# Two pairs' first rows at the head of an attention and feed-forward kernel on one core

## The chip, the cores and the metric

The kernel runs on 1 core of one Trainium2 chip. The metric is device microseconds of one execution, the median of several. TensorE's clock is shown by the profile as the share that the throttle granted, 1.00 for 2.4 GHz and 0.50 for 1.2 GHz.

## What is computed

The attention has 4 batches, 8 heads, 576 positions and 64 columns to a head. A decay that follows from `f` is added to the scores, so that each position fades with distance:

```python
log_f = np.log(np.clip(f, 0.0001, 1.0))
cum = np.cumsum(log_f, axis=-1)
scores = scale * q @ k.T + cum[:, :, :, None] - cum[:, :, None, :]   # then the causal mask
attn = softmax(scores);  x = (attn @ v) laid out as 2304 rows of 512
x = relu(x @ w_in1)**2 @ w_out1          # 512 -> 2048 -> 512
x = elu(x @ w_in2) @ w_out2              # 512 -> 2048 -> 512
```

## The kernel before

All four stages are in one program. The attention is done two heads (a pair) at a time. A pair has five steps, which the list `todo` holds: `("A", 0)` and `("A", 1)` are the first 256 rows of its two heads, `("4", 0)` the last 64 rows of both heads together, and `("B", 0)` and `("B", 1)` the 256 rows between, for one head each. Here A00 is step A of pair 0, head 0, and B11 is step B of pair 1, head 1. A step has a first half, `soft` (scores on TensorE, row minimum on VectorE, exponentials on ScalarE with their sums) and a second half, `outs` (transposes of the exponentials on TensorE, copies of them on ScalarE, the product with the values, and after the second head of a pair the division by the sums, `norm_x`, and the split of the result, `store_x`). `LAG = 1` puts the second half one turn of the loop behind the first.

Batch 0 is "plain": its scores are one fp32 product over 68 rows, 64 of q and k and 4 that carry the decay. Those four rows are the decay rows. For the 256 first rows they are taken straight from the tile `ca`; for the other rows they go out to the DRAM tensor `aug` (`aug_rows`, five writes) and are read back into the operand tiles. Of each batch 0 head the kernel loads q and k (320 KB), values (160 KB) and decay rows (20 KB); of pair 0 it loads ahead of that a 256 KB piece, `first`, and a 128 KB piece, `firstv`, which is what its A steps need.

The first feed-forward layer's weights come as 64-bit numbers in 16 pieces of 512 KB. `stage` asks for the next piece, and `words` turns one into fp32: an absolute value on ScalarE (L150), four operations on VectorE (L151 to L154), then a rounding copy on ScalarE (L170) and a subtraction on VectorE (L119). `W_AT` says how many pieces are converted in each turn of the loop. 256 tokens at a time (a unit) go through that layer, and its matmuls are put between the attention's steps by a running credit (`fill`). Unit 0 can begin when the last A step of batch 0 is done and converted weights are there; its first matmul in the profile is at 91.74 us.

All loads and stores go by the queue of SyncE. `queued` ties each of batch 0's loads behind the one before it, so that their order is the program's. The order of the rest on each engine comes from a planner that runs when the program is built; `issue_after` adds ties to it. Engines take their instructions in the order so made.

While unit 0 hasn't begun, `fill` gives TensorE products of a zero tile (L255): 46 of them at the very start, and two or three after each half step in the first `FILL_TO` turns, which makes 54 more in the kernel before. Buffers that matter: `raw` has 3, `ea` (exponentials of A) 2, `eb` (exponentials of B) 3, `xA` one. The tiles `cp` and `cn`, from which `aug_rows` writes, hold two of the three `eb` buffers until turn 8 (`AUG1`), when the rows of the other batches are written.

Of the kernel before, what the change touches and what calls it, by code (L numbers as in the profile page):

```python
# [22 lines left out]
Q0, Q4 = 448, 320  # L23
QW = 704
RAW = QW + S
ALL = RAW + 5 * D
# [6 lines left out]
W_MAX = float(np.uint32(0x47EFFE00).view(np.float32))  # L33
PACE = (1.5, 1.5, 1.5, 1.5)
COST = {'A': 0.7, '4': 1.1, 'B': 1.7}
W_AT = (1, 1, 0, 1, 1, 0, 0, 1, 2, 1, 0, 0, 1, 2, 1, 0, 0, 1, 2, 1)
AHEAD = 2
FETCH = 4
LAG = 1
HOLD = 8  # L40
KEPT = 0

PLAIN = (0,)

# [11 lines left out]
OPS = 7  # L56


WARM, FILL, FILL_TO = 46, 2, 6
AUG1 = 8  # L60
DELAY = 0
MEM = "gpsimd"
# [7 lines left out]
def f32(ap):  # L70
    return ap.bitcast(F32)
# [10 lines left out]
def attention_then_moe_kernel(ctx, tc, first, firstv, plain, qkv, aug0, f, w1, w2, out):  # L82
    nc = tc.nc
# [11 lines left out]
    aug = dram.tile([B * H, 4, RAW], F32, name="aug")  # L95
# [36 lines left out]
        nc.gpsimd.tensor_tensor(out=dst, in0=x, in1=f32(hi), op=ALU.subtract)  # L132

    staged = []
    to_stage = [(fc, i) for i in range(2) for fc in range(8)]

    def stage():
        if not to_stage:
            return
        fc, i = to_stage.pop(0)  # L140
        n = n_raw[0] % 5
        n_raw[0] += 1
        raw = raws_w[:, n] if n < 2 else a1.tile([128, 512, 2], I32, tag="qk2", name="wraw1", bufs=3)
        queued(raw, w1[fc, i].bitcast(I32).rearrange("p (n t) -> p n t", t=2), len(to_stage) > 10)
        staged.append(raw)

    def words(raw):
        lo, hi = raw[:, :, 0], raw[:, :, 1]
        t = xa.tile([128, 512], I32, tag="o", name="wt")
        nc.scalar.activation(out=f32(t), in_=f32(hi), func=AF.Abs)  # L150
        nc.vector.tensor_scalar(f32(t), f32(t), W_MIN, W_MAX, op0=ALU.max, op1=ALU.min)  # L151
        nc.vector.tensor_scalar(t, t, 3, 0x3FFFFFFF, op0=ALU.logical_shift_left, op1=ALU.bitwise_and)
        nc.vector.scalar_tensor_tensor(t, hi, -0x40000000, t, op0=ALU.bitwise_and, op1=ALU.bitwise_or)  # L153
        nc.vector.scalar_tensor_tensor(t, lo, 29, t, op0=ALU.logical_shift_right, op1=ALU.bitwise_or)  # L154
        return t
# [102 lines left out]

    raws = {}

    pairs = {}

    def fetch_head(b, h, part):
        if b in PLAIN:
            fetch_plain(b, h, part)
# [7 lines left out]
    def queued(out, in_, hold=True):  # L273
        if last_dma[0] is None:
            last_dma[0] = nc.sync.dma_start(out=out, in_=in_)
            return
        with tc.issue_after(last_dma[0].ins):
            d = nc.sync.dma_start(out=out, in_=in_)
        if hold:
            last_dma[0] = d  # L280

    def fetch_first(t):
        queued(t[0:64, 0:1024], first)
        stage()
        for i in range(2):
            queued(t[64:68, 512 * i:512 * i + 512], f32(ca[i:i + 1]))
        queued(t[:, 1024:1280], firstv)

    def fetch_plain(b, h, part):
        g = b * H + h  # L290
        k = h % 2
        if part == "A":
            if k == 0:
                t = ab.tile([128, ALL], F32, tag="raw", name="rawA", bufs=BUFS["raw"])
                fetch_first(t)
                pairs[b, h // 2] = t
            t = pairs[b, h // 2]
            raws[b, h, part] = Plain(t, 512 * k - Q0, 512 * k + 256, t[:, 1024 + 128 * k:1152 + 128 * k].rearrange("p (j d) -> p j d", d=D))
            return
        if k == 0:  # L300
            t = ab.tile([128, ALL], F32, tag="raw", name="rawB", bufs=BUFS["raw"])
            v = t[:, RAW:ALL]
        else:
            t = hd.tile([128, RAW], F32, tag="qk1", name="rawC", bufs=BUFS["qs"])
            v = hd.tile([128, 5 * D], F32, tag="vv", name="vp", bufs=BUFS["vv"])
        queued(t[0:64, 0:RAW], plain[h])
        queued(v, qkv[b, h, :, RAW:ALL])
        if g >= 2:
            nc.sync.dma_start(out=t[64:68, 0:RAW], in_=aug[g])
        else:  # L310
            late_aug.append((t, g))
        raws[b, h, part] = Plain(t, 0, QW, v.rearrange("p (j d) -> p j d", d=D))

    late_aug = []

    def aug_split():
        cp, cn = (ab.tile([32, 2, S - 256], F32R, tag="eb", name=t, bufs=BUFS["eb"]) for t in ("cp", "cn"))
        split_c(cp, cn, slice(256, S))
        return cp, cn
# [54 lines left out]
        nc.vector.tensor_tensor_reduce(out=e, in0=s, in1=m, scale=-0.125, scalar=init, op0=ALU.add, op1=ALU.min, accum_out=nm)  # L374

    def expo(e, nm, z):
        nc.scalar.activation(out=e, in_=e, func=AF.Exp, bias=nm, scale=-1.0, accum_out=z)

    def invert(z, r):
        nc.vector.tensor_scalar(z, z, 1e-9, None, op0=ALU.add)  # L380
# [56 lines left out]
    def tr(dst, src, c0=0):  # L437
        seen[0] = nc.tensor.transpose(dst, src, ident[:, c0:c0 + 128])  # L438
# [33 lines left out]
    def store_x(b, hp, x, c0, n):  # L472
# [224 lines left out]
    loads = []  # L697
    for i, (b, hp, kind, k) in enumerate(todo):
        if (b, hp) == (0, 0):
            if kind == "A":  # L700
                loads.append((i, b, hp, k, "A"))
            elif kind == "4":
                loads += [(i + 2, b, hp, 0, "B"), (i + 2, b, hp, 1, "B")]
        elif kind == "A":
            loads.append((i, b, hp, k, "F"))

    fetches = [(i if part == "F" else 0, b, 2 * hp + k, part) for i, b, hp, k, part in loads]

    def ready(u):
        b, s = divmod(u * CH + CH - 1, S)  # L710
# [477 lines left out]
```

## Time and profile before

| | |
|---|---|
| three runs | 1048.82, 1050.67, 1051.39 us; median 1050.67 |
| profiled execution | 1046.67 us, its span 1044.8 us, granted clock 0.99 on average |
| busy share of the span | TensorE 98%, VectorE 67%, ScalarE 50%, GpSimd 26% |
| zero products (L255) | 100, the first at 1.05 us, the last at 53.2 us |
| first scores of A00, of the step 4 of pair 0, of unit 0 | 10.0, 21.3, 91.7 us |

TensorE is busy nearly throughout by this account, but the ends of matmuls are modelled, and a slice in which it runs at half clock counts as busy too. So the share of an engine has to be read with the number of its instructions and with the granted clock, and for each stretch by itself.

### The profile page before, as it was taken

To read this page: it belongs to the slowest core of one execution; us is meant where nothing else is said; L and a number is where in the kernel's file an instruction comes from. 1 tells how busy PE (TensorE), PEld (TensorE's weight loads), DVE (VectorE), ACT (ScalarE), POOL (GpSimd) and SP (SyncE) were. 2 spreads that over 40 slices of the span, in tenths; PEclk is the share of its full clock that TensorE was granted. 3 is DMA by queue.
4 is the path that set the end of the run, shared out by engine and by line. 5 is a ranking of instruction groups with operands and counts; after the bars stand their busy time and mean duration, and the time that the engine had idled before them with its cause. 6 is when DMAs were issued, how large, how long until landed. Compare 5 with 4: busy or idle time off the path is not lost.

```text
span 1044.8 us, 17562 instructions
## 1 busy us (share of the span) xinstructions
PE 1025.5 (98%) x6372; PEld 903.4 (86%) x6372; DVE 702.9 (67%) x1569; ACT 526.1 (50%) x1207; POOL 267.2 (26%) x284
## 2 busy tenths in 40 slices
PE   7999999999999999999999999999999999999998
PEld 6655899999999998889988888988998988899987
DVE  5799478686876338756384869886454989745554
ACT  3677667676767425433253544464343565433331
POOL 2137768777764230004011240210000000000000
PEclk8799999999999999999999999999999999999999
DMA  6955643645441173435264565644324464544502
GB/s 180 244 155 160 191 147 118 189 161 164 155 150 51 42 246 105 127 91 191 76 207 152 190 222 184 216 166 182 101 81 141 143 239 144 162 155 119 171 21 81
DMA packets 73161, 157.23 MB, mean 150 GB/s; under 512 B 9196, under 2 KB 34156, under 8 KB 73044
## 3 DMA queue, kind: packets, MB, share of 16 engines
q1 hardware_dynamic: 73076, 156.13, 46.5%
q8 instruction: 50, 0.82, 0.3%
q14 instruction: 35, 0.29, 0.1%
HBM read 113.98 MB, written 39.22 MB: 147 GB/s over the span
## 4 chain that ended last, share of the span: by engine, by line
PE 84%; DVE 8%; DMA 3%; issue 1%; ACT 1%; POOL 1%; SPq 0%; ACTq 0%; DVEq 0%; POOLq 0%
PE O L183 29%; PE P L183 15%; PE pH L183 11%; PE o L183 7%; PE ph L183 6%; PE pt L438 4%; PE pv L445 4%; PE s L366 2%; PE s L370 2%; PE s L371 2%; PE pv L442 2%; DMA x<-yl 1%; DVE wt L154 1%; DVE wt L153 1%; PE idle L255 1%
## 5 line engine op out<-in xcount | busy, mean ns | idle before, releaser
L183 PEld LDWEIGHTS P<-xu,v 128*128 128x128 f32 x1536 | 200.5, 189 | 11.2 <-DMA xu<-x 1.1
L183 PE MATMUL P<-xu,v 128*128 128x256 f32 x1536 | 204.0, 282 | 0.7 <-DMA xu<-x 0.7
L183 PE MATMUL O<-v,gh 128*128 128x512 f32 x576 | 169.2, 393 | 1.0 <-ACT gh L1003 1.0
L183 PE MATMUL pH<-xu,w 128*128 128x512 f32 (+1 forms) x672 | 140.9, 360 | 0.0
L183 PEld LDWEIGHTS pH<-xu,w 128*128 128x128 f32 x672 | 113.8, 188 | 19.9
L183 PE MATMUL O<-gh,w 128*128 128x512 f32 (+1 forms) x448 | 122.2, 362 | 0.0
L183 PEld LDWEIGHTS O<-v,gh 128*128 128x128 f32 x576 | 102.9, 188 | 18.8 <-ACT gh L1003 1.2
L183 PE MATMUL O<-v,gl 128*128 128x512 f32 x288 | 100.9, 393 | 0.0
L183 PEld LDWEIGHTS O<-gh,w 128*128 128x128 f32 x448 | 79.8, 189 | 14.0
L1032 ACT ACTIVATE hs<-P 128x256 f32<-128x256 f32 x128 | 48.1, 380 | 83.3 <-PE P L183 82.7
L132 POOL TENSOR_TENSOR yl<-pr,yh 128x512 fp32r<-128x512 f32 x18 | 24.5, 1361 | 246.2 <-ACT yh L852 169.9
L132 POOL TENSOR_TENSOR qk<-raw,qk 64x576 fp32r<-64x576 f32 (+1 forms) x48 | 77.7, 1619 | 21.5 <-DVE qk L127 9.7
L1035 DVE TENSOR_TENSOR hs<-P,hs 128x256 f32<-128x256 f32 x96 | 40.4, 422 | 59.6 <-PE P L183 57.4
L183 PE MATMUL O<-gl,w 128*128 128x512 f32 (+1 forms) x224 | 79.9, 363 | 0.0
L183 PE MATMUL o<-gh,w 128*128 128x256 f32 x384 | 75.6, 289 | 0.0
L183 PE MATMUL ph<-xu,w 128*128 128x256 f32 x480 | 67.4, 287 | 0.7 <-ACT g L605 0.7
L1057 ACT ACTIVATE g<-g 128x512 f32<-128x512 f32 x64 | 40.2, 628 | 54.2 <-DVE g L1049 32.3
L610 ACT ACTIVATE gh<-g 128x512 fp32r<-128x512 f32 (+1 forms) x80 | 46.8, 586 | 39.9 <-DVE g L609 35.9
L609 DVE TENSOR_TENSOR g<-g 128x512 f32<-128x512 f32 (+1 forms) x56 | 44.1, 787 | 31.0 <-ACT g L605 30.8
L1003 ACT ACTIVATE gh<-g 128x512 fp32r<-128x512 f32 x72 | 45.4, 631 | 34.4 <-DVE g L1058 27.5
L183 PEld LDWEIGHTS ph<-xu,w 128*128 128x128 f32 x480 | 60.9, 191 | 1.2 <-ACT g L605 0.9
L183 PEld LDWEIGHTS O<-v,gl 128*128 128x128 f32 x288 | 52.8, 188 | 9.9
(155 smaller groups left out, 2067.2 us busy)
## 6 DMA issues: line engine op xcount, KB each, us to landing
xu<-x SPq DMA_DIRECT2D x66, 512.0 KB
wraw<-in_w_dram SPq DMA_DIRECT2D x57, 512.0 KB
raw<-in_qkv_dram SPq DMA_DIRECT2D x24, 800.0 KB
x<-yh SPq DMA_DIRECT2D x31, 256.0 KB
x<-yl SPq DMA_DIRECT2D x31, 256.0 KB
x<-xs SPq DMA_DIRECT2D x16, 320.0 KB
xu<-x SPq DMA_DIRECT2D x16, 256.0 KB
raws_w<-in_w_dram SPq DMA_DIRECT2D x7, 512.0 KB
```

The lines of the kernel that those rows point to most:

```text
L132: nc.gpsimd.tensor_tensor(out=dst, in0=x, in1=f32(hi), op=ALU.subtract)
L183: nc.tensor.matmul(out=dst, lhsT=l, rhs=r, start=first and i == 0, stop=last and i == n - 1, skip_group_check=skip)
L366: seen[0] = nc.tensor.matmul(out=dst, lhsT=hh.t[0:68, hh.q + q0:hh.q + q0 + 128], rhs=hh.t[0:68, hh.k + j0:hh.k + j0 + n], start=first, st ...
L370: nc.tensor.matmul(out=dst, lhsT=qk1[:, q0:q0 + 128], rhs=qk1[:, QW + j0:QW + j0 + n], start=first, stop=False)
L438: seen[0] = nc.tensor.transpose(dst, src, ident[:, c0:c0 + 128])
L445: seen[0] = nc.tensor.matmul(out=dst, lhsT=hh[2][:, J, :], rhs=hl[i], start=first and i == 0, stop=last and i == 1)
L609: (nc.vector if sq == "v" else nc.gpsimd).tensor_tensor(out=g[:, 0:n], in0=g[:, 0:n], in1=g[:, 0:n], op=ALU.mult)
L610: nc.scalar.activation(out=gh[:, 0:n], in_=g[:, 0:n], func=AF.Copy)
L1003: nc.scalar.activation(out=gh, in_=g, func=AF.Copy)
L1032: nc.scalar.activation(out=o, in_=x, func=AF.Copy)
L1035: nc.vector.tensor_tensor(o, y, x, op=ALU.add)
L1057: nc.scalar.activation(out=gs[i], in_=gs[i], func=AF.Exp)
```

## The change

The A steps of two pairs (`EARLY = 2`) come first, then steps 4, B, B of pair 0 and of pair 1; the other pairs keep their order. To feed that, `first` and `firstv` are held for both pairs (the host concatenates them), and the start is written out in `fetch_start`: loads that wait for no computation stand ahead of the decay rows of A, and the second piece of weights ahead of the q, k and values of head 1. `W_AT` is spread differently, with the same 16 pieces in the first 20 turns and 8 of them in the first ten; the absolute value of a piece (L150) is tied behind the last exponentials traced before it; the transposes in `norm_x` of batch 0 are tied behind the last matmul traced; and the zero products stop after four turns of the loop instead of six.

```diff
-W_AT = (1, 1, 0, 1, 1, 0, 0, 1, 2, 1, 0, 0, 1, 2, 1, 0, 0, 1, 2, 1)
+W_AT = (1, 0, 1, 0, 1, 1, 1, 1, 1, 1, 0, 1, 1, 1, 1, 0, 1, 1, 1, 1)
+EARLY = 2
-WARM, FILL, FILL_TO = 46, 2, 6
+WARM, FILL, FILL_TO = 46, 2, 4
@@ words
-        nc.scalar.activation(out=f32(t), in_=f32(hi), func=AF.Abs)
+        if last_exp[0] is None:
+            nc.scalar.activation(out=f32(t), in_=f32(hi), func=AF.Abs)
+        else:
+            with tc.issue_after(last_exp[0].ins):
+                nc.scalar.activation(out=f32(t), in_=f32(hi), func=AF.Abs)
@@ fetch_first, fetch_plain
-    def fetch_first(t):
-        queued(t[0:64, 0:1024], first)
-        stage()
-        for i in range(2):
-            queued(t[64:68, 512 * i:512 * i + 512], f32(ca[i:i + 1]))
-        queued(t[:, 1024:1280], firstv)
+    def load_a(t, hp):
+        queued(t[0:64, 0:1024], first[hp])
+    def rows_a(t, hp):
+        for i in range(2):
+            queued(t[64:68, 512 * i:512 * i + 512], f32(ca[2 * hp + i:2 * hp + i + 1]))
+    def values_a(t, hp):
+        queued(t[:, 1024:1280], firstv[hp])
+    def load_b(h):
+        t, v = whole[h]
+        queued(t[0:64, 0:RAW], plain[h])
+        queued(v, qkv[0, h, :, RAW:ALL])
+    def rows_b(h):
+        queued(whole[h][0][64:68, 0:RAW], aug[h])
+    def fetch_start():
+        queued(aug[0:H], aug0[0:H])
+        ta = tile_a(0)
+        load_a(ta, 0)
+        stage()
+        values_a(ta, 0)
+        tb = tile_a(1)
+        load_a(tb, 1)
+        tile_b(0)
+        load_b(0)
+        values_a(tb, 1)
+        rows_a(ta, 0)
+        rows_a(tb, 1)
+        stage()
+        tile_b(1)
+        load_b(1)
+        aug_rows(slice(0, H), *cpn)
+        stage()
+        for h in range(2):
+            rows_b(h)
+        while len(staged) < 5:
+            stage()
@@ expo
-        nc.scalar.activation(out=e, in_=e, func=AF.Exp, bias=nm, scale=-1.0, accum_out=z)
+        last_exp[0] = nc.scalar.activation(out=e, in_=e, func=AF.Exp, bias=nm, scale=-1.0, accum_out=z)
@@ norm_x
-            tr(pr[:, i * 128:i * 128 + 128], rb[:, i])
+            if b == 0:
+                with tc.issue_after(seen[0].ins):
+                    tr(pr[:, i * 128:i * 128 + 128], rb[:, i])
+            else:
+                tr(pr[:, i * 128:i * 128 + 128], rb[:, i])
@@ todo, loads
-    todo = [(b, hp, kind, k) for b in range(B) for hp in range(H // 2)
-            for kind, k in (("A", 0), ("A", 1), ("4", 0), ("B", 0), ("B", 1))]
+    both, rest = (("A", 0), ("A", 1)), (("4", 0), ("B", 0), ("B", 1))
+    todo = [(0, hp, *s) for part in (both, rest) for hp in range(EARLY) for s in part]
+    todo += [(b, hp, *s) for b in range(B) for hp in range(H // 2) for s in both + rest if b or hp >= EARLY]
-        if (b, hp) == (0, 0):
+        if b == 0 and hp < EARLY:
...
@@ the loop, turn 0
-            queued(aug[0:H], aug0[0:H])
             cpn = aug_split()
+            fetch_start()
...
-        if i == 0:
-            stage()
-            aug_rows(slice(0, H), *cpn)
-            for t, g in late_aug:
-                queued(t[64:68, 0:RAW], aug[g])
-            while len(staged) < 5:
-                stage()
```

## Rows read from the trace of the kernel before

**Rows 1.** Stretch, length, busy us of PE, PEld, DVE, ACT, POOL; clock, DMA share, GB/s

```profile
9.98:21.32 11.34, 6.94 (x35) 4.78 (x35) 5.88 (x17) 4.83 (x15) 0.60 (x2) 0.93 0.68 165
21.32:38.43 17.11, 17.11 (x51) 12.06 (x51) 8.55 (x23) 7.26 (x16) 2.00 (x2) 0.55 1.03 260
38.43:91.74 53.31, 51.86 (x248) 31.20 (x247) 48.94 (x130) 40.92 (x110) 20.12 (x24) 1.00 0.63 190
...
110.00:300.00 190.00, 187.23 (x1472) 179.99 (x1472) 138.97 (x403) 131.13 (x355) 141.40 (x146) 1.00 0.51 157
```

**Rows 2.** Waits of VectorE from 10 to 92 us, the longest

```profile
DVE wt L151 <- ACT wt L150: 6.4, 2, 3.6
```

**Rows 3.** Timeline of ScalarE: start us, us, what, idle before and its releaser

```profile
6.99 0.67 ACT L150 ACTIVATE wt<-raws_w 128x512 f32<-128x512 f32 x1
...
17.96 0.66 ACT L150 ACTIVATE wt<-raws_w 128x512 f32<-128x512 f32 x1 [3.49 <-DMA raws_w<-in_w_dram]
...
18.79 0.47 ACT L123 ACTIVATE ea<-pt 128x384 f32<-128x384 f32 x1
```

**Rows 4.** Timeline of all engines, the decay rows and what they release

```profile
7.91 1.41 SPq L278 DMA_DIRECT2D rawA<-ca  x2
...
10.01 1.10 PE L366 MATMUL s<-rawA 68*128 68x256 f32 x4 [0.96 <-DMA rawA<-ca]
...
14.83 0.27 SPq L278 DMA_DIRECT2D aug<-cn  x1
...
18.98 0.25 SPq L278 DMA_DIRECT2D rawB<-aug  x1
...
21.32 2.26 PE L366 MATMUL s<-rawB 68*128 68x288 f32 x4 [0.90 <-DVE xA L470]
```

**Rows 5.** Chain of waits from 18 to 26 us, in order of time

```profile
18.65 0.44 DVE wt L151
...
20.30 0.69 DVE wt L154
...
21.34 4.16 PE s L366 x8
```

**Rows 6.** Busy time and clock in stretches of 2 us, columns as in rows 1

```profile
8.00:10.00 2.00, 1.05 (x9) 0.86 (x9) 1.93 (x7) 0.00 (x0) 0.00 (x0) 1.00 0.02 6
...
14.00:16.00 2.00, 1.95 (x11) 1.15 (x10) 0.18 (x1) 0.47 (x3) 0.60 (x2) 1.00 1.05 234
...
18.00:20.00 2.00, 0.69 (x3) 0.54 (x4) 1.28 (x3) 1.25 (x3) 0.00 (x0) 0.94 0.03 8
...
34.00:36.00 2.00, 2.00 (x12) 2.00 (x10) 0.18 (x1) 0.45 (x2) 0.00 (x0) 0.50 1.01 182
36.00:38.00 2.00, 2.00 (x10) 1.37 (x10) 0.85 (x2) 1.93 (x4) 0.00 (x0) 0.79 1.12 200
```

**Rows 7.** Timeline of VectorE: first row minimum of B00 and of B01

```profile
28.73 0.69 DVE L374 CUSTOM_DVE_ANT_0 eb<-s,mz 128x512 f32<-128x512 f32 x1 [1.85 <-PE s L366]
...
38.43 0.69 DVE L374 CUSTOM_DVE_ANT_0 eb<-s,mz 128x512 f32<-128x512 f32 x1 [0.54 <-PE pt L438]
```

**Rows 8.** Groups by line, 10 to 92 us: busy us, mean ns of one, idle before

```profile
L374 DVE CUSTOM_DVE_ANT_0 eb<-s,mz 128x512 f32<-128x512 f32 (+1 forms) x13 | 7.9, 623 | 3.5 <-PE s L366 3.0 <-PE pt L438 0.5
...
L377 ACT ACTIVATE ea<-ea,nm 128x256 f32<-128x256 f32 (+1 forms) x16 | 7.1, 448 | 1.4 <-DVE nm L374 1.4
...
L374 DVE CUSTOM_DVE_ANT_0 ea<-s,mz 128x256 f32<-128x256 f32 (+1 forms) x16 | 5.1, 349 | 0.9 <-PE s L366 0.9
...
L377 ACT ACTIVATION_READ_ACCUMULATOR ea<-ea,nm 128x1 f32 x16 | 3.1, 192 | 0.0
...
L123 ACT ACTIVATE ea<-pt 128x384 f32<-128x384 f32 x6 | 2.9, 479 | 1.1 <-PE pt L438 1.1
...
L123 ACT ACTIVATE xA<-pv 64x256 f32<-64x256 f32 x6 | 2.2, 367 | 1.3 <-PE pv L442 1.2
...
L374 DVE CUSTOM_DVE_ANT_0 e<-s,m,nm 128x288 f32<-128x288 f32 x4 | 2.0, 503 | 0.0
```

More of the change, by code (lines that the diff above doesn't have):

```diff
@@ L134, in attention_then_moe_kernel @@
     staged = []
+    last_exp = [None]
     to_stage = [(fc, i) for i in range(2) for fc in range(8)]
@@ L259, in attention_then_moe_kernel @@
     raws = {}
-    pairs = {}
     def fetch_head(b, h, part):
         if b in PLAIN:
-            fetch_plain(b, h, part)
+            fetch_plain(h)
             return
@@ L280, in queued @@
             last_dma[0] = d
-    def fetch_first(t):
-        queued(t[0:64, 0:1024], first)
-        stage()
-        for i in range(2):
-            queued(t[64:68, 512 * i:512 * i + 512], f32(ca[i:i + 1]))
-        queued(t[:, 1024:1280], firstv)
[L289 to L300, printed above, removed]
+    whole = {}
@@ new lines, in tile_a @@
+    def tile_a(hp):
+        t = ab.tile([128, ALL], F32, tag="raw", name="rawA", bufs=BUFS["raw"])
+        for k in range(2):
+            raws[0, 2 * hp + k, "A"] = Plain(t, 512 * k - Q0, 512 * k + 256,
+                                             t[:, 1024 + 128 * k:1152 + 128 * k].rearrange("p (j d) -> p j d", d=D))
+        return t
+    def load_a(t, hp):
+        queued(t[0:64, 0:1024], first[hp])
+    def rows_a(t, hp):
+        for i in range(2):
+            queued(t[64:68, 512 * i:512 * i + 512], f32(ca[2 * hp + i:2 * hp + i + 1]))
@@ L301, in fetch_plain, with tile_b @@
+    def values_a(t, hp):
+        queued(t[:, 1024:1280], firstv[hp])
+    def tile_b(h):
+        if h % 2:
+            t = hd.tile([128, RAW], F32, tag="qk1", name="rawC", bufs=BUFS["qs"])
+            v = hd.tile([128, 5 * D], F32, tag="vv", name="vp", bufs=BUFS["vv"])
+        else:
             t = ab.tile([128, ALL], F32, tag="raw", name="rawB", bufs=BUFS["raw"])
             v = t[:, RAW:ALL]
-        else:
-            t = hd.tile([128, RAW], F32, tag="qk1", name="rawC", bufs=BUFS["qs"])
-            v = hd.tile([128, 5 * D], F32, tag="vv", name="vp", bufs=BUFS["vv"])
+        whole[h] = t, v
+        raws[0, h, "B"] = raws[0, h, "F"] = Plain(t, 0, QW, v.rearrange("p (j d) -> p j d", d=D))
@@ L306, in fetch_plain @@
+    def load_b(h):
+        t, v = whole[h]
         queued(t[0:64, 0:RAW], plain[h])
[L307 to L314, printed above, removed]
+        queued(v, qkv[0, h, :, RAW:ALL])
[23 more added lines that the diff above has]
+            stage()
@@ L316, in aug_split, with fetch_plain @@
+    def fetch_plain(h):
+        tile_b(h)
+        load_b(h)
+        rows_b(h)
     def aug_split():
@@ L468, in norm_x @@
         for i in range(2):
-            tr(pr[:, i * 128:i * 128 + 128], rb[:, i])
+            if b == 0:
+                with tc.issue_after(seen[0].ins):
+                    tr(pr[:, i * 128:i * 128 + 128], rb[:, i])
+            else:
+                tr(pr[:, i * 128:i * 128 + 128], rb[:, i])
         nc.vector.tensor_tensor(x[:, c0:c0 + 256], x[:, c0:c0 + 256], pr[:, 0:256], op=ALU.mult)
@@ L692, in weights @@
             yield
-    todo = [(b, hp, kind, k) for b in range(B) for hp in range(H // 2)
-            for kind, k in (("A", 0), ("A", 1), ("4", 0), ("B", 0), ("B", 1))]
+    both, rest = (("A", 0), ("A", 1)), (("4", 0), ("B", 0), ("B", 1))
+    todo = [(0, hp, *s) for part in (both, rest) for hp in range(EARLY) for s in part]
+    todo += [(b, hp, *s) for b in range(B) for hp in range(H // 2) for s in both + rest if b or hp >= EARLY]
     loads = []
+    fetches = []
     for i, (b, hp, kind, k) in enumerate(todo):
-        if (b, hp) == (0, 0):
+        if b == 0 and hp < EARLY:
             if kind == "A":
@@ L702, in attention_then_moe_kernel @@
             elif kind == "4":
-                loads += [(i + 2, b, hp, 0, "B"), (i + 2, b, hp, 1, "B")]
+                loads += [(i + AHEAD, b, hp, k, "B") for k in range(2)]
+                if hp:
+                    fetches += [(i, b, 2 * hp + k, "B") for k in range(2)]
         elif kind == "A":
             loads.append((i, b, hp, k, "F"))
-    fetches = [(i if part == "F" else 0, b, 2 * hp + k, part) for i, b, hp, k, part in loads]
+            fetches.append((i, b, 2 * hp + k, "F"))
     def ready(u):
@@ L1169, in weights, with paired @@
         return np.stack([a, np.asarray(wo).reshape(NF, 128, 512)], axis=1).view(np.int64)
+    def paired(a):
+        return np.ascontiguousarray(a.reshape(-1, 2, *a.shape[1:]).transpose(0, 2, 1, 3)).reshape(len(a) // 2, a.shape[1], -1)
     arrays = {
-        "in_first_dram": np.concatenate([qkv[0, h, 0:64, Q0:QW + 256] for h in range(2)], axis=1),
-        "in_firstv_dram": np.concatenate([qkv[0, h, :, RAW:RAW + 2 * D] for h in range(2)], axis=1),
+        "in_first_dram": paired(qkv[0, 0:2 * EARLY, 0:64, Q0:QW + 256]),
+        "in_firstv_dram": paired(qkv[0, 0:2 * EARLY, :, RAW:RAW + 2 * D]),
         "in_plain_dram": np.ascontiguousarray(qkv[0, :, 0:64, 0:RAW]),
```

## The prediction

> **What bounds the kernel now.** I read the page's forty slices first, then busy time by stretch, then the waits and the chain of waits of the first 110 us, because the change touches only these. From 110 us on TensorE is busy for 187 of 190 us at full clock and no other engine comes near [rows 1]. That part is a fixed amount of TensorE work: whatever moves its start moves the end by the same amount. So the question is how much sooner batch 0 and the 16 pieces of weights are done, which is when unit 0 can begin (91.7 us).
>
> The reader is to see three stretches there [rows 1]. From 38.4 to 91.7 us VectorE is busy for 48.9 of 53.3 us, 92%: it is the bound. From 21.3 to 38.4 it has only 8.6 us of work in 17.1 us; TensorE fills that stretch wholly, at a mean clock of 0.55. From 10.0 to 21.3 it has 5.9 us in 11.3 us, and no engine is full. The idle time of VectorE, 5.5 and 8.6 us, is all that the change can win, since after it the engine is nearly full already.
>
> Why the first of these is idle is shown by the waits: VectorE waited 6.4 us for the absolute value of a piece of weights, 3.6 us of it at once [rows 2]. ScalarE had met the absolute value of the second piece at its head and stood 3.49 us until 17.96 us, when the piece landed; the copy of transposed exponentials behind it, which has nothing to do with weights, went at 18.79 us [rows 3]. TensorE had no work from about 16.0 to 19.3 us, and its clock fell from 1.00 within the slice from 18 to 20 us [rows 6]. It stayed at 0.50 until the slice from 36 to 38 us, so the second stretch is long because of the first. In the chain of waits TensorE is the bound from 21.34 us on, with 4.16 us for the scores of step 4 alone [rows 5].
>
> **The change part by part.** *The start.* The decay rows of A were asked for at 7.91 us, with no transfers before them (6 GB/s in that slice), and the first scores began at 10.0 us [rows 4, 6]. Now 992 KB stand ahead of them that need not wait: values of pair 0 (128), q and k of pair 1 (256), plain q, k and values of head 0 (480), values of pair 1 (128). At the 234 GB/s of the slice from 14 to 16 us [rows 6] this is 4.3 us. What was asked for before had landed by 6.99 us, when ScalarE began on the first piece [rows 3], so the backlog ends between 10.0 (no gap at all between the two) and 11.3 us. I take the scores 0.8 us later; if small rows overtake, 0; with 2 us for the rows after the backlog, 2.
>
> *A of pair 1 comes in.* Four A steps now run where two did. By ScalarE's queue each costs 2 x 0.448 + 2 x 0.192 + 0.479 + 0.367 = 2.13 us [rows 8]; two more are 4.3 us, which is as much as the wait that goes (3.5 us) plus a little. The absolute value is tied behind exponentials of A01 and meets a piece that has landed, for the second piece is asked for four row transfers after 7.91 us, about 10.7 us, and needs some 2.2 us. New waits: `xA` has one buffer, so A10's copy into it, and on ScalarE all behind it, waits until pair 0's result is split, and `ea` has two, so A10's minimum waits for A00's product. I put the first scores of step 4 at 21.7 us, 0.4 us later than now; between 19.0 (when its decay rows can be there, next part) and 24.0 us (all the work of ScalarE ahead of it, without overlap).
>
> *The decay rows of step 4.* They were asked for at 18.98 us, 4.15 us after the last of the writes that they read back, and SyncE's queue stood behind that wait, with 8 GB/s moved between 18 and 20 us [rows 4, 6]. In the new order the writes begin at about 12.3 us, behind the second piece and head 1 (992 KB, 4.3 us by the rate above), and the third piece of weights is asked for ahead of the rows; they should land at about 19 us, hidden by A of pair 1. If that cover is thinner than I think, TensorE idles again. Behind the rows on the queue stand two more pieces and all loads of pair 1's B steps, which now have 10 us more until they are needed.
>
> *Step 4 and B00 at full clock.* This is the main term. From step 4's first scores to B01's first minimum took 17.1 us (21.3 to 38.4; B01's minimum waits for the last transposes of B00, its `eb` buffer) [rows 7]. The TensorE work is half of that at full clock, 8.6 us, and some zero products in it go as well. VectorE's work in it is two operations of step 4 at 0.503, two minima at 0.623, and two pieces of weights, four operations from 18.65 to 20.99 us and a subtraction of some 0.7, so 1.0 + 1.25 + 2 x 3.0 = 8.3 us [rows 5, 8]. Both run side by side; at the 92% of the later stretch VectorE needs 9.0 us. I take 10.0, for the stretch is a chain across four engines. Gain 7.1 us; bounds 8.8 (17.1 - 8.3) and 0 (the clock falls as before).
>
> *The rest.* Two A steps' minima leave the stretch that VectorE bounds: 4 x 0.349 = 1.4 us, 1.5 us at 92% [rows 1, 8]. A little of the fourth piece that was done by 38.4 us isn't now. I take 1.0, bounds 0 and 1.6.
>
> *What costs nothing.* The zero products end after turn 3: by `fill`'s counts 3 + 7 + 7 + 7 = 24 instead of 54 after the first 46. They are fillers, and their only effect is on the clock (a rival, below). 16 pieces stay 16, with 8 in the first ten turns either way. The tie of the two transposes in `norm_x` keeps them behind work that they can only follow; if a division is late for it, that is hidden by the next A. The 384 KB more to load are 1.7 us of transfers spread over a start that had idle transfers [rows 6].
>
> **Sum.** -0.4 + 7.1 + 1.0 = 7.7 us (the 0.8 us are in the first term). The profiled execution took 1046.67 us, 1.87 us more than its span, so its like would take 1039.0; it lies 4.0 us under the median of the runs, 1050.67, and against that the forecast is 1043.0. Bounds: step 4 at 24.0 with no other gain, 2.7 us slower; step 4 at 19.0 with 8.8 and 1.6, 12.7 us faster.
>
> **The rivals.** *First: the clock falls all the same, and what is won is small.* Step 4's rows go through DRAM, and the old pause from the last write to the request was 4.15 us [rows 4]; with bigger transfers ahead it could be longer. If TensorE runs out of A work for some 2 or 3 us before they land, step 4 and B00 go at half clock again. Left are -0.4 + 1.0 = 0.6 us: 1050. Against it: four A steps, 24 zero products between them, and ScalarE as their bound keep TensorE occupied to about 21 us.
>
> *Second: slower, because the half clock lasts.* The place is step 4 to B11. The clock came back at about 36.4 us, 15 us after TensorE's work was again without gaps, while it did the transposes of B00 with zero products between them [rows 5, 6]. In the new kernel no zero products follow turn 3. If the clock falls before step 4 and only returns behind pair 1, the excess of the second stretch (17.1 - 8.3 = 8.8 us) is paid a second time, for B01 to B11 is more than as much TensorE work: 8.8 - 0.6 = 8 us slower, 1059. It is slower than before from the point where the half clock lasts to about B01's end, and by more than 0.3% (3.2 us, about what a measurement here can tell from no change) beyond that. Against it: from 53 us on the clock stood at 1.00 with no zero products at all, with A, 4 and B steps mixed [rows 1].
>
> The Trainium skill ("TensorE: Matmul & The Clock Gate", section "Part 1: The HAM clock gate") says that the clock is halved after an idle spell and given back after sustained work soon afterwards. By that page a fall would cost step 4's scores alone, about 2 us, and the time would be 1045 in both of these cases; the trace shows the fall as the page has it, but not the quick return, and so I let the trace's 15 us set both prices.
>
> *Third: more is won.* If VectorE never waits from 12 us on, the bounds above meet: 11 to 13 us, 1038 to 1040. Against it: the single free `eb` buffer and ScalarE's A queue.
>
> **How the numbers follow.** The clock holds and the sum stands within its bounds: 0.65, with 1038.5 to 1047 as its own range. First rival 0.17, second 0.11, third 0.07. Predicted 1043.0. The range runs from 1037.5 to 1051.5: it takes in the sum, the third and the first, and leaves out the second and some mishap of the planner's order. Faster by over 0.3% are the sum and the third, less the part of the sum's lower bound that is too small to tell: 0.70. Within 0.3% are the first rival and that part: 0.18. Slower: 0.12.
>
> **What would show it.** Right: no wait of ScalarE of over 1 us for a piece of weights before 20 us; granted clock 1.00 in every slice from 10 to 40 us; A00's scores at 10.5 to 11.5, step 4's at 20 to 23, B01's first minimum at 29 to 34, unit 0's first matmul at about 84 us, and the same distance from there to the end. Wrong: a gap of TensorE ahead of step 4 with slices of 0.50 behind it; or all early marks earlier and unit 0 not, which would mean that something else than VectorE bounds the stretch after 38 us.

## The result and the profile after

The changed kernel took 1038.95 us (median of 6, 1037.27 to 1044.1) beside 1048.9 us for the kernel before (median of 6). The ratio is 0.9909 with an interval of 0.9882 to 0.9935, so 0.9% faster: 9.5 us, between 6.8 and 12.4. The profiled execution took 1038.02 us with a span of 1036.2 us and a mean granted clock of 0.995. The rows below compare it with the profiled execution before, which took 1046.67 us.

Stretches of the kernel after, columns as in [rows 1]: from A00's first scores to step 4's, from there to B01's first minimum, from there to unit 0's first matmul, and the long stretch behind.

```profile
11.08:19.83 8.75, 8.75 (x52) 7.27 (x53) 5.78 (x24) 6.35 (x20) 0.80 (x2) 1.00 0.77 204
19.83:31.38 11.55, 11.46 (x55) 6.62 (x53) 10.82 (x28) 9.56 (x25) 3.22 (x5) 1.00 1.02 278
31.38:83.02 51.64, 46.98 (x204) 26.87 (x204) 41.06 (x111) 37.02 (x96) 13.98 (x19) 0.93 0.70 201
110.00:300.00 190.00, 186.89 (x1490) 182.61 (x1490) 144.06 (x421) 133.31 (x363) 142.88 (x154) 1.00 0.50 157
```

Against [rows 1] the first stretch is 8.75 us long where it was 11.34, with the first halves of two more A steps in it; their second halves come behind step 4's first scores. The second is 11.55 where it was 17.11, at clock 1.00 where it was 0.55, and VectorE is busy for 10.82 us of it. The third is 51.64 where it was 53.31. Unit 0 begins at 83.02 us in place of 91.74, and from there to the end of the span it is 953.2 us where it was 953.1: what the start won arrives at the end whole.

The third stretch holds something new. VectorE is busy for 41.06 us of it in place of 48.94, but it is idle for 10.6 us where it was idle for 4.4, and the clock is 0.93. Timeline of ScalarE, then of SyncE, of VectorE and of TensorE of the kernel after (start us, us, what, idle before and its releaser):

```profile
13.99 0.51 ACT L412 ACTIVATE ea<-ea,nm 128x256 f32<-128x256 f32 x1 [0.17 <-DVE nm L409]
...
14.88 0.65 ACT L156 ACTIVATE wt<-raws_w 128x512 f32<-128x512 f32 x1
15.44 0.47 ACT L124 ACTIVATE ea<-pt 128x384 f32<-128x384 f32 x1
```

```profile
7.91 2.67 SPq L282 DMA_DIRECT2D rawA<-ca  x4
10.62 0.44 SPq L282 DMA_DIRECT2D raws_w<-in_w_dram  x1
...
13.80 0.26 SPq L282 DMA_DIRECT2D aug<-cn  x1
14.62 0.36 SPq L282 DMA_DIRECT2D wraw<-in_w_dram  x1
17.46 0.25 SPq L282 DMA_DIRECT2D rawB<-aug  x1
...
44.20 0.75 SPq L282 DMA_DIRECT2D aug<-ca  x2
44.99 0.77 SPq L282 DMA_DIRECT2D aug<-cp  x2
```

```profile
31.38 0.68 DVE L409 CUSTOM_DVE_ANT_0 eb<-s,mz 128x512 f32<-128x512 f32 x1
...
46.95 0.69 DVE L409 CUSTOM_DVE_ANT_0 eb<-s,mz 128x512 f32<-128x512 f32 x1 [3.67 <-DMA aug<-cp]
```

```profile
11.08 1.13 PE L401 MATMUL s<-rawA 68*128 68x256 f32 x4 [1.79 <-DMA rawA<-ca]
...
19.83 0.65 PE L401 MATMUL s<-rawB 68*128 68x288 f32 x2
...
23.71 0.86 PE L477 MATMUL pv<-ea,rawA 128*64 128x256 f32 x4
...
26.45 0.86 PE L477 MATMUL pv<-ea,rawA 128*64 128x256 f32 x4
...
47.70 2.08 PE L401 MATMUL s<-rawB 68*128 68x256 f32 x4 [3.23 <-DVE nm L409]
```

The absolute value of the second piece (L150 before, L156 now) goes at 14.88 us without a wait, where it stood 3.49 us [rows 3]. The decay rows of step 4 are read back from 17.46 us on, 3.66 us after the last write, and TensorE comes to them at 19.83 us without a wait. The products of A10 and A11 with the values run at 23.71 and 26.45 us, so behind step 4's scores. But B11's first minimum at 46.95 us waits 3.67 us for writes of decay rows: the tile that it fills is held by `cp` until those writes are done, and they are asked for in turn 8, at 44.20 us. TensorE stands 3.23 us for it. Granted clock of the kernel after in stretches of 2 us, columns as in [rows 6]:

```profile
14.00:16.00 2.00, 2.00 (x14) 1.72 (x13) 0.77 (x4) 1.91 (x6) 0.55 (x2) 1.00 1.03 224
18.00:20.00 2.00, 2.00 (x15) 1.54 (x14) 1.43 (x7) 1.95 (x7) 0.00 (x0) 1.00 0.50 92
34.00:36.00 2.00, 1.09 (x5) 0.89 (x6) 0.30 (x1) 1.23 (x4) 0.20 (x1) 1.00 1.02 199
46.00:48.00 2.00, 0.29 (x1) 0.30 (x2) 1.05 (x3) 0.31 (x1) 0.00 (x0) 0.91 0.60 105
48.00:50.00 2.00, 2.00 (x5) 1.17 (x5) 1.25 (x5) 1.62 (x5) 0.20 (x1) 0.50 0.97 332
...
54.00:56.00 2.00, 2.00 (x10) 1.23 (x9) 0.15 (x1) 0.00 (x0) 0.00 (x0) 0.89 1.06 344
```

The slices from 8 to 46 us stand at 1.00. From 44.47 to 47.70 us TensorE has nothing to do (0.29 us of work in the slice from 46 to 48), the clock falls, and it is back in the slice from 54 to 56.

### The profile page after: what moved, and what is told of

It reads as the page before. It is cut to its first block, busy times and chain, and to the rows that moved or that the text cites. A ratio compares the mean times of both kernels' runs of the same rounds, so it can differ in the third digit from the quotient of the medians.

```text
span 1036.2 us, 17514 instructions
## 1 busy us (share of the span) xinstructions
PE 1014.7 (98%) x6342; PEld 895.5 (86%) x6342; DVE 707.8 (68%) x1569; ACT 526.4 (51%) x1207; POOL 264.1 (25%) x284
## 4 chain that ended last, share of the span: by engine, by line
PE 72%; DVE 6%; POOL 2%; DMA 2%; issue 2%; ACT 1%; ACTq 0%; POOLq 0%; DVEq 0%; SPq 0%
PE O L189 29%; PE P L189 16%; PE pH L189 11%; PE o L189 5%; PE ph L189 4%; PE pv L480 3%; PE pt L473 2%; DMA x<-yl 1%; PE s L405 1%; PE s L406 1%; POOL qk L133 1%; DVE v L120 1%; DVE pr L950 0%; DVE g L648 0%; DVE eb L409 0%
```

## The experiments

Twelve kernels were run, each beside the kernel before on the same chip. The quotes name the theories by letters. In short, one reading was that of the prediction, that the gain comes from the wait for the second piece and from the clock that falls in it; its rivals were the tie of the weights, the order of the steps by itself, the zero products, and the late decay rows of the other batches. This table holds every run; the last three columns are of the one profiled execution of each, and its clock differs from execution to execution.

| kernel | median us (runs) | ratio, interval | half clock before 60 us | unit 0's first matmul | span |
|---|---|---|---|---|---|
| before | see above | 1 | 20 to 36 | 91.7 | 1044.8 |
| the change | 1038.95 (6) | 0.9909, 0.9882 to 0.9935 | 48 to 55 | 83.0 | 1036.2 |
| `tie_alone` | 1048.58 (12) | 1.0007, 0.9989 to 1.0026 | 11 to 15, 21 to 35 | 90.5 | 1044.3 |
| `loads_alone` | 1042.8 (6) | 0.9932, 0.9907 to 0.9956 | 11 to 38 | 91.2 | 1046.1 |
| `steps_alone` | 1037.76 (6) | 0.9896, 0.9873 to 0.9919 | 12 to 19 | 80.9 | 1034.1 |
| `before_bridge` | 1041.63 (6) | 0.9933, 0.9913 to 0.9952 | 11 to 17, 28 to 34 | 87.1 | 1042.9 |
| `after_early1` | 1042.3 (8) | 0.9945, 0.9922 to 0.9967 | 20 to 36 | 91.0 | 1045.6 |
| `after_fill0` | 1044.84 (12) | 0.9966, 0.9948 to 0.9984 | 14 to 40 | 88.5 | 1044.2 |
| `after_fill6` | 1041.9 (6) | 0.9923, 0.9901 to 0.9945 | 12 to 22, 49 to 56 | 87.6 | 1041.0 |
| `after_aug4` | 1038.46 (5) | 0.9896, 0.9874 to 0.9919 | 12 to 24 | 85.8 | 1036.6 |
| `after_warm56` | 1039.2 (6) | 0.9916, 0.9882 to 0.9949 | 12 to 25 | 82.3 | 1041.3 |
| `after_warm56_aug4` | 1041.7 (10) | 0.9936, 0.9912 to 0.9961 | 15 to 24 | 85.1 | 1037.2 |
| `steps_warm52_aug4` | 1038.19 (11) | 0.9913, 0.9886 to 0.9941 | 25 to 31 | 85.1 | 1035.2 |
| `after_no_tie` | 1040.37 (12) | 0.9948, 0.9917 to 0.9980 | 12 to 23 | 91.4 | 1043.3 |

In all 14 profiles the span less unit 0's first matmul is 950 to 959 us (953.1 before), so the end follows the start of unit 0 to within 9 us. And the clock falls at least once before 60 us in every one of them, the change included.

**The tie and `W_AT` alone**, on the kernel before:

```diff
-W_AT = (1, 1, 0, 1, 1, 0, 0, 1, 2, ...
+W_AT = (1, 0, 1, 0, 1, 1, 1, 1, 1, ...
@@ words
+            with tc.issue_after(last_exp[0].ins):
+                nc.scalar.activation(out=f32(t), in_=f32(hi), func=AF.Abs)
```

> The kernel before with one part of the change alone: absolute values tied behind exponentials, with the new spread of the weight pieces over the turns. Theory A (the gain is the kept clock plus the A steps of pair 1 in idle time): the second piece still lands at about 17.9 us and its absolute value still stands ahead of the second copy of A's transposes, so ScalarE stands for 3 us, TensorE idles and the clock falls: ratio to before 0.997 to 1.003. Theory B (the tie removes the wait by itself): ratio 0.991 to 0.994, no wait of ScalarE over 1 us before 20 us.

1.0007, no difference: in the old order of loads the piece still lands late (ScalarE stands 3.13 us for it, until 18.53 us), and unit 0 begins at 90.5 us. The tie by itself brings nothing.

**The order of the loads alone**, with the steps in their old order:

```diff
+        load_a(ta, 0); stage(); values_a(ta, 0)
+        tile_b(0); load_b(0)
+        rows_a(ta, 0)
+        stage()
+        tile_b(1); load_b(1)
+        aug_rows(slice(0, H), *cpn)
         ... (the third piece, then the decay rows of step 4)
```

> The kernel before with the loads' order alone (values of pair 0 and q, k, values of head 0 ahead of the decay rows of A, the second weight piece ahead of head 1's, the third ahead of the decay rows of step 4). Theory A: the second piece lands at 12 to 13 us, ScalarE's wait goes, but with two A steps TensorE is out of work from about 16 us until step 4's rows land at 18 to 19 us; step 4 starts some 2 us sooner than 21.3 us and the clock may fall: ratio 0.994 to 0.999. Theory C (the loads' order is the whole gain): ratio 0.990 to 0.992, clock 1.00 from 10 to 40 us.

0.9932, about 7 us. Its six executions run from 1037.59 us at a mean clock of 0.997 to 1048.13 us at 0.986. The profiled one is the slowest of them and shows the half clock from 11 to 38 us, so its trace doesn't show where the others won.

**The order of the steps alone**, with the old `W_AT`, no ties, zero products in six turns, and pair 1's A loads put behind pair 0's:

```diff
+EARLY = 2
@@ fetch_start
+        tb = tile_a(1)
+        load_a(tb, 1); rows_a(tb, 1); values_a(tb, 1)
         ... (the rest in the order of before)
```

> The kernel before with the order of steps alone: A of two pairs first, the loads in the old order with those of pair 1's A steps behind those of pair 0's, no tie, old spread of weights, zero products in six turns. Theory A: the second piece is asked for behind 2.1 MB and lands at about 20 us, ScalarE meets it with two A steps undone, and step 4's rows land at 22 to 24 us; the clock falls or not by the length of that gap; ratio 0.994 to 1.002. Theory D (the order of steps is the whole gain): ratio 0.990 to 0.992.

0.9896: the whole gain, by theory D's number; theory A's 0.994 to 1.002 is missed. This is the run that changes the reading, since the ties are not in it, and of the loads that go ahead only those that A of pair 1 needs. Stretches of this kernel around its fall of the clock, columns as in [rows 6]:

```profile
12.00:14.00 2.00, 1.81 (x7) 1.36 (x6) 1.25 (x5) 1.77 (x9) 0.00 (x0) 0.50 0.61 147
...
18.00:20.00 2.00, 2.00 (x11) 1.31 (x10) 0.18 (x1) 0.78 (x2) 0.00 (x0) 0.80 0.74 272
20.00:22.00 2.00, 2.00 (x16) 1.71 (x16) 0.61 (x5) 1.62 (x6) 0.00 (x0) 1.00 0.01 3
```

The half clock falls on A steps here and is over before step 4 and B00. Step 4's first scores come at 23.57 us, later than before, and B01's first minimum at 35.03 us, 3.4 us sooner. The larger part of the 10.8 us by which unit 0 is sooner is won behind that, in the stretch to unit 0, which took 53.31 us before:

```profile
35.03:80.90 45.87, 43.50 (x197) 24.81 (x198) 40.60 (x110) 35.42 (x95) 15.76 (x19) 1.00 0.70 213
```

**The clock alone**, on the kernel before: 13 zero products between A01's transposes and its last product with the values, which cover the pause of 16 to 19 us (three that stood behind this half step are left out, so ten more in all). Row of the kernel before, columns as in [rows 6]:

```profile
16.00:18.00 2.00, 0.03 (x1) 0.00 (x0) 0.00 (x0) 0.04 (x1) 0.00 (x0) 1.00 0.67 255
```

```diff
+            bridge = k and not bridged
+            if bridge:
+                with tc.issue_after(seen[0].ins):
+                    seen[0] = busy(13)
```

> The kernel before with 13 more zero products put between the last transposes and the last product of A01, so that TensorE isn't idle while it waits for ScalarE from 16.0 to 19.3 us; nothing else moves. Theory A (the clock is the main term): granted clock 1.00 from 16 to 40 us, the stretch from step 4's first scores to B01's first minimum 10 to 12 us instead of 17.1, ratio 0.994 to 0.996. Rival (the second stretch is long for another reason, the one eb buffer or the weights): clock 1.00 and the stretch still over 15 us, ratio 0.999 to 1.001.

0.9933: about 7.0 us (0.0067 x 1048.2) for products that compute nothing, the size of the prediction's main term. From 18 to 22 us the clock of its profiled execution, the slowest of the six, is 1.00, where it fell before [rows 6]. But theory A's trace isn't met: the clock is at half from 11 to 17 and again from 28 to 34 us, within B00, and from step 4's first scores to B01's first minimum it took 14.57 us (20.99 to 35.56) in place of 17.1, where 10 to 12 were expected. So the 7.0 us are what filling that pause is worth, with a clock that still fell elsewhere. VectorE's idle time from 10 us to unit 0's first matmul is 11.9 us (77.13 less 65.26 busy), where by the first three of [rows 1] it was 18.4 (81.76 less 63.37). Rows of this kernel:

```profile
18.00:20.00 2.00, 2.00 (x20) 2.00 (x18) 1.55 (x3) 0.96 (x3) 0.00 (x0) 1.00 0.10 29
...
28.00:30.00 2.00, 1.45 (x5) 0.85 (x3) 1.97 (x5) 1.30 (x4) 1.11 (x1) 0.50 1.03 260
...
10.00:87.13 77.13, 74.42 (x342) 48.24 (x342) 65.26 (x167) 53.41 (x140) 24.07 (x29) 0.91 0.72 213
```

**The change without the two pairs** (loads, ties, `W_AT` and four turns of zero products stay, A of pair 1 goes back to its place):

```diff
-EARLY = 2
+EARLY = 1
@@ fetch_start
-        tb = tile_a(1)
-        load_a(tb, 1)
-        values_a(tb, 1)
-        rows_a(tb, 1)
```

> The changed kernel with EARLY = 1: the loads' order, the tie, the new spread of weights and four turns of zero products stay; steps of pair 0 then pair 1 as before. Theory A (clock and moved work are separate terms): the clock may hold or fall, no A work is moved in, 3 to 7 us faster than before, ratio 0.993 to 0.997. Theory C (loads and tie together are the gain): ratio 0.990 to 0.992.

0.9945, so 5.8 us against 9.5: by the medians some 4 us of the gain need the two pairs, though the intervals just overlap. In its profile TensorE waits 2.92 us for step 4's decay rows, at 18.57 us, and the clock stands at 0.50 from 20 to 36 us: the cover that the prediction asked of A of pair 1 is gone. This execution is the slowest of its eight.

**No zero products behind the first 46**, and **zero products in six turns as before**:

```diff
-WARM, FILL, FILL_TO = 46, 2, 4
+WARM, FILL, FILL_TO = 46, 2, 0      # after_fill0
+WARM, FILL, FILL_TO = 46, 2, 6      # after_fill6
```

> The changed kernel without any zero product after the first 46. Theory G (the 24 products keep the clock in the A steps): the clock falls between 10 and 25 us and stays at half for 10 us or more, 4 to 8 us slower than the changed kernel, ratio to before 0.995 to 1.000. Rival H (the A steps of two pairs hold the clock by themselves): ratio 0.989 to 0.993.

> The changed kernel with zero products in six turns, as before the change. If their end was a loss (clock lower from 25 us on): faster than the changed kernel by 1 to 3 us, ratio to before 0.987 to 0.990. If they are free or not needed there, as the prediction has it: ratio 0.989 to 0.993. If they stand in the way of the products behind them: slower by 1 to 3 us, 0.993 to 0.995.

Without them 0.9966: nearly two thirds of the gain is lost (9.5 to 3.6 us), by theory G. The clock of the profiled execution stands at 0.50 from 14 to 40 us, and that of all twelve is 0.975 to 0.989 on average. In six turns the new order of the steps makes ten more of them (80 in all against 70, not the 100 of the kernel before): 0.9923, no difference from the change that can be told. So the 24 do as well as 34, and that they end after turn 3 cost nothing that these runs can tell.

**The decay rows of the other batches in turn 4**, which frees `cp` and `cn` sooner:

```diff
-AUG1 = 8
+AUG1 = 4
```

> The changed kernel, with the decay rows of the other batches written in turn 4 instead of 8. In the changed kernel VectorE waits 3.7 us for these writes at B10 (they free the eb buffers) and TensorE's clock falls behind that wait, from 47.8 to 55.3 us. Theory E (that wait is the next bound): the wait goes, no fall there, 3 to 6 us faster than the changed kernel, ratio to before 0.985 to 0.989. Rival F (VectorE is the bound from there on anyway, or the 480 KB copy delays the loads of pair 1): ratio 0.989 to 0.993.

0.9896: by its interval the same as the change. The wait is gone (timeline of VectorE of this kernel, B11's first minimum):

```profile
48.06 0.68 DVE L409 CUSTOM_DVE_ANT_0 eb<-s,mz 128x512 f32<-128x512 f32 x1
```

It goes without idle time, but in this profiled execution all was later already, since the clock was at half from 12 to 24 us. What the 3.67 us are worth in the median can't be told from this run: by the two intervals taken together it lies between 2 us lost and 5 us won.

**More zero products at the start**, to close the pause ahead of A00's scores, by itself, with the edit before, and on the order of the steps alone:

```diff
-WARM, FILL, FILL_TO = 46, 2, 4
+WARM, FILL, FILL_TO = 56, 2, 4      # after_warm56, after_warm56_aug4
+WARM, FILL, FILL_TO = 52, 2, 6      # steps_warm52_aug4
-AUG1 = 8
+AUG1 = 4                            # the last two
```

> The change with 56 zero products ahead of A00's scores in place of 46, so that TensorE has no pause between the last of them (9.3 us) and the first scores (11.1 us). Theory H (in some executions the clock falls at about 11.5 us because of that pause, and this is what spreads the times of one kernel by 4 to 7 us): no execution falls then, all granted clocks are 0.992 or more, and the ratio is 0.985 to 0.989, 1 to 4 us under the change itself. Theory I (the spread of the clock comes from elsewhere, or the later pauses decide): clocks and ratio as the change's, 0.989 to 0.993. In the trace by both: scores of A00 at 11.1 to 11.4 us, with TensorE idle under 0.5 us before them.

> As before, and the rows of the other batches written in turn 4 in place of turn 8, so that the buffers of B10 and B11 are free when they are wanted. Theory H with the wait at 46.95 us as the cause of the fall from 47.8 to 55.3 us: both pauses are gone, the clock stays at 1.00 from 8 to about 98 us, average 0.995 or more, ratio 0.983 to 0.988. Theory I: as the change, 0.989 to 0.992, and the second edit worth nothing again, as the first alone showed (0.9896).

> The order of the steps alone (old order of the loads, old W_AT, no ties, zero products in six turns), with 52 zero products at the start and the rows of the other batches in turn 4. Theory D (the order of the steps carries the whole gain) with H: A00's scores at 10.0 to 10.3 us without a pause before them, no fall of the clock from 8 to 98 us, ratio 0.980 to 0.986, the best of all. By theory D without H: 0.988 to 0.992, as the order of the steps alone (0.9896).

0.9916, 0.9936 and 0.9913: theory H's numbers are missed, and none of the three beats the change. Nor did they test it: the pauses weren't closed. Timeline of TensorE of `after_warm56`:

```profile
1.05 8.55 PE L261 MATMUL idle<-zero 128*128 128x256 f32 x56 [1.05 <-DVE zero L256]
```

```profile
12.18 1.22 PE L401 MATMUL s<-rawA 68*128 68x256 f32 x2 [2.58 <-DMA rawA<-ca]
```

Ten more had been priced at some 0.18 us each, the mean of the 46 (8.23 us). But the products go at two speeds: by their starts in the trace they are 0.21 us apart at first and 0.12 us later, so the ten at the end fill 1.2 us, and the decay rows landed 1.1 us later in this execution as well. Whether the early fall comes from that pause stays open.

**Without the tie of the absolute value**:

```diff
-            with tc.issue_after(last_exp[0].ins):
-                nc.scalar.activation(out=f32(t), in_=f32(hi), func=AF.Abs)
+            nc.scalar.activation(out=f32(t), in_=f32(hi), func=AF.Abs)
```

> The change without the tie of the pieces' absolute values behind exponentials; the planner then places the second piece's absolute value ahead of A01's exponentials on ScalarE. Theory J (the tie is needed here, unlike in the kernel before, since it is asked for at 10.6 us and lands at about 14.5): ScalarE waits 1 to 3 us for the piece with A01's exponentials behind it, unit 0's first matmul 1 to 3 us later, ratio 0.992 to 0.996. Theory K (the tie does nothing here either, the wait is covered by zero products and the later A steps): ratio 0.989 to 0.992, as the change.

0.9948, but with twelve executions in two groups: seven from 1037.99 to 1040.49 us at clocks of 0.990 to 0.993, and five from 1045.31 to 1050.97 us at 0.980 to 0.984. The wait is there, smaller than theory J had it (timeline of ScalarE of this kernel):

```profile
14.98 0.66 ACT L153 ACTIVATE wt<-raws_w 128x512 f32<-128x512 f32 x1 [0.94 <-DMA raws_w<-in_w_dram]
15.55 0.49 ACT L412 ACTIVATE ea<-ea,nm 128x256 f32<-128x256 f32 x1
```

A01's first exponentials go at 15.55 us where the change has them at 13.99. The seven are as fast as the change, so without the tie the gain is there in some executions. Whether it keeps executions out of the slower group can't be told: the interval reaches from 0.9917 to 0.998. (Unit 0 at 91.4 us in its profile has a second half clock ahead of it, from 67 to 84 us.)

## Why the prediction was right, and where its steps were not

1043.0 us was predicted against 1050.67. The ratio of 0.9909 makes 1041.1 of that, so 9.5 us were won and 7.7 forecast. The profiled execution gives 8.65 (1046.67 less 1038.02), against 1039.0 forecast for its like. By its three stretches it won 1.5, 5.6 and 1.7 us where -0.4, 7.1 and 1.0 were forecast. That the sum is so close is in part luck, for three misses cancel in it.

Of the signs that it named this execution shows all but one: step 4's scores came at 19.83 us and not between 20 and 23. But it has the highest clock of the six, 0.995 beside 0.988 to 0.992, and two of the others were as fast (1037.46 us at 0.990, 1037.27 at 0.992). So among the six the gain doesn't go with the mean clock, and where the clock fell in the other five no trace shows. Term by term, by the profiled execution:

**The start** held: scores of A00 at 11.08 us, 10.8 forecast.

**A of pair 1 comes in** was too dear. Step 4's first scores are at 19.83 us, within the bounds, where 21.7 was taken; +1.5 us in place of -0.4. The prediction put two whole A steps, 4.3 us of ScalarE, ahead of step 4. In fact only their first halves are there: ScalarE is busy for 6.35 us in the stretch where it was 4.83, and their products with the values run at 23.71 and 26.45 us, in the next one, where ScalarE is busy for 9.56 us in place of 7.26. Of the new waits on `xA` and `ea` only 0.57 us shows, of A11's minimum for a product, at 19.18 us. The decay rows of step 4 were asked for 3.66 us behind the last write and TensorE's matmuls didn't wait for them (a weight load did, for 0.27 us), so that cover held.

**Step 4 and B00 at full clock**, the main term, has the sign and the mechanism right and was sized too high in this execution: 17.1 to 11.55 us, +5.6 in place of +7.1. The clock stayed at 1.00 and VectorE is busy for 94% of the stretch, with 10.82 us of work and not 8.3: three pieces of weights fell into it where two had been counted. (TensorE is listed as busy for 11.46 us of it, so that VectorE is its bound isn't shown.) Lines of VectorE in the stretch, kernel after (count | busy us, mean ns | idle before):

```profile
L159 DVE SCALAR_TENSOR_TENSOR wt<-wraw,wt 128x512 int32<-128x512 int32 x3 | 2.1, 686 | 0.0
L120 DVE TENSOR_TENSOR w<-wt,w 128x512 fp32r<-128x512 f32 x3 | 2.0, 681 | 0.0
L158 DVE TENSOR_SCALAR wt<-wt 128x512 int32<-128x512 int32 x3 | 2.0, 654 | 0.1
```

That isn't lost, since a piece that is done here isn't left for the next stretch. As for the clock's worth by itself, `before_bridge` measured 7.0 us, with the falls named above. In most of the other kernels with the new order the stretch takes as little, 11.46 us in `steps_alone`, `after_aug4` and `after_warm56`, only later: the half clock fell ahead of it.

**The rest** was mis-sized: 1.0 us forecast, 1.7 in this execution, 7.4 in `steps_alone` (53.31 less 45.87). The reason is one that the prediction excluded. It said that the idle time of VectorE is all that the change can win. From A00's first scores to unit 0's first matmul VectorE was busy for 63.4 of 81.8 us [rows 1] and is now busy for 57.7 of 71.9. So 9.8 us less, of which 4.1 are idle time and 5.7 are work, 1.1 of these for the later first scores alone; that leaves the 8.7 us of unit 0. In both kernels 16 minima of A steps and 13 of B steps are in it; what is less is weights: 14 subtractions (L119 before, L120 now) ahead of unit 0 before, 13 now, and 12 in `steps_alone`, whose `W_AT` is the old one. One piece is some 3 us by the prediction's price. The remainder is that the same operations took less time, the shift (L152 before, L158 now) 0.507 us on average in place of 0.635; why is not shown. VectorE's slack behind unit 0 takes the piece, for from 110 to 300 us TensorE is busy for 186.9 of 190 us, and the distance to the end is unchanged. So it isn't so that a fixed amount of VectorE's work stands ahead of unit 0.

It is the order of the steps that does it. From B01's first minimum to unit 0 VectorE is busy for 48.3 to 49.0 us in the five kernels with the old order, and for 40.6 to 42.7 us in eight of the nine with the new one (45.3 in `after_no_tie`, whose stretch has the second half clock). But that VectorE's work is what counted there is argued, not shown: less of it ahead of unit 0 can also follow from an earlier unit 0. TensorE has less to do in that stretch too, 46.98 us where it had 51.86. And the prediction read VectorE as the bound from 38.4 us on from its busy share, while the chain of waits of the kernel before runs through TensorE up to 66.4 us, zero products included up to 53.6 us, then through a load, and only from 72.6 us on mostly through VectorE:

```profile
52.91 0.67 PE idle L255 x4
...
66.40 6.19 DMA raw<-in_qkv_dram
```

The zero products aren't what made that stretch long: `after_early1` has its last one at 28.4 us, and the stretch takes 54.9 us there (with a half clock from 74 to 78 us in it).

In the change the stretch holds 41.1 us of VectorE's work where it held 48.9, which by itself would have won some 8 us (the prediction had 1.0); the new wait for `cp`, other pauses and the half clock from 48 to 55 us took 6.2 of these back. In `after_warm56`, where that stretch ran at full clock, it is 9.5 us shorter than before (row of this kernel):

```profile
38.55:82.34 43.79, 43.37 (x204) 25.89 (x204) 41.17 (x111) 36.72 (x96) 15.61 (x20) 1.00 0.68 216
```

In that execution B01's first minimum is at 38.55 us, as late as before (38.43, [rows 7]), after a half clock from 12 to 25 us that fell on A steps; step 4 and B00 then run at full clock, from 27.09 us on. Yet unit 0 begins at 82.3: by B01's first minimum two A steps more are done. That is the second way in which the change wins. It stands even where the prediction's first rival comes true, step 4 and B00 at half clock, for which 0.6 us of gain were left. The profile of `after_fill0` shows that case: step 4's first scores at 22.60 us and B01's first minimum at 41.57, with the clock at 0.50 from 14 to 40 us. B01 is 3.1 us later than before and unit 0 3.2 us sooner, and the median of its twelve executions is 3.6 us ahead. So the rival's price was wrong too, by the same term. Stretches of `after_fill0`, columns as in [rows 6]:

```profile
28.00:30.00 2.00, 2.00 (x6) 1.15 (x5) 1.16 (x5) 1.59 (x4) 0.00 (x0) 0.50 1.00 174
...
38.00:40.00 2.00, 1.69 (x7) 0.93 (x6) 0.92 (x2) 1.13 (x3) 0.00 (x0) 0.50 0.74 198
```

**What costs nothing** was right for the end of the zero products after turn 3, as far as `after_fill6` can tell. The 24 that are left do count, as the prediction had it where it named them against its first rival: `after_fill0` shows that they carry some 6 us.

**The new waits** were sought at `xA`, `ea` and the decay rows of step 4, and the one that came was at a buffer named in the kernel's description: `cp` and `cn` hold two `eb` buffers until turn 8. Their writes come at the same time as before (44.2 us), while B11's minimum now wants the buffer some 43 us into the run. The prediction counted that buffer against the third rival and not in the sum.

**The second rival**, slower by a lasting half clock, came in no run of the new order: the longest half clock seen there, 14 to 40 us in `after_fill0`, still gave 0.9966.

The Trainium skill ("TensorE: Matmul & The Clock Gate", section "Part 1: The HAM clock gate") says that what the chip looks at to set this clock isn't aligned with a kernel's start, so that one kernel meets the transition at other points from run to run. The traces agree: the zero products at the start, which begin at 1.05 us in each, speed up from one in 0.21 us to one in 0.12 us within the slice from 4 to 6 us in `after_warm56` and within the next in the change. Zero products (L261) in stretches of 2 us, first of the kernel after, then of `after_warm56` (TensorE, weight load; clock, DMA share, GB/s; a product that reaches over an edge counts on both sides):

```profile
4.00:6.00 2.00, 2.00 (x11) 2.00 (x11) 1.00 1.00 319
6.00:8.00 2.00, 2.00 (x16) 2.00 (x16) 1.00 1.12 289
```

```profile
4.00:6.00 2.00, 2.00 (x16) 2.00 (x16) 1.00 1.00 308
6.00:8.00 2.00, 2.00 (x19) 2.00 (x18) 1.00 1.11 271
```

The granted clock reads 1.00 at both speeds there, so the starts of the products tell more than that column; at a granted clock of 0.50 the chain of waits of the kernel before has 7 of them in 1.49 us, the same 0.21 us each. The quick return that the Trainium skill has there is seen in one place and not in another: 7 us in `steps_alone` (12 to 19) and in the change (48 to 55), but 16 us before and 26 us in `after_fill0`, in both with TensorE listed as busy for nearly all of it.

What stays open: how the gain of a median execution divides between the clock and the work that moved. `before_bridge` gives 7.0 us for the clock in the old order, and `steps_alone` 10.9 us with an early fall in its profile, so they don't simply add; `loads_alone` reaches 7 by another way, which its profile doesn't show. And it stays open which engine's work it is that the new order takes out of the way of unit 0.

## What to carry to other kernels

Ask of the engine that bounds a start not only where it idles but which of its work has to be done by then at all: work that can go behind the point where another engine becomes the bound may be won whole (from B01 to unit 0 up to 9.5 us were won, where VectorE had idled for 4.4 us; which engine's work made it isn't shown). Check a bound read from busy shares against the chain of waits. Put steps with little work for TensorE where the pauses are, and those that fill it behind them, so that a half clock falls on the first. When steps move forward by 9 us, list every buffer that is freed by turn number, for those turns don't move with them.

## What the runs showed of the chip that was not expected

One kernel's executions differ by 13 us with its granted clock: `after_no_tie` took 1037.99 us at 0.993 and 1050.97 at 0.982, and `loads_alone` 1037.59 at 0.997 and 1048.13 at 0.986. After much the same pause ahead of A00's scores the clock fell at about 12 us in one profile (`steps_alone`, 1.40 us idle) and not in another (the change, 1.79 us idle). So a trace shows the clock of one execution, and a term that hangs on it has to be sized by several executions.
